# Forgetting attention and a GELU MLP on one core: four-head value products, weights loaded behind the first v, first scores by pairs of heads

## The chip, the cores and the metric

The kernel runs on one core of a Trainium2 chip. The metric is device time in microseconds (us). It is compared with the time of the kernel before the change on the same inputs. Engine names are those of the profile: PE is TensorE (PEld its weight loads), DVE is VectorE, ACT is ScalarE, POOL is GpSimd, SP is SyncE. SPq and POOLq are the sequencers of SP and POOL, which issue DMAs.

## The reference

Attention with a forget gate over 8 batches of 8 heads, 576 positions and 64 dims per head, followed by an MLP on the 4608 tokens, 512 wide, 2048 inside:

```python
scores = scale * np.matmul(q, k.transpose(0, 1, 3, 2))
log_f = np.log(np.clip(f, 0.0001, 1.0))
cum = np.cumsum(log_f, axis=-1)
decay = cum[:, :, :, None] - cum[:, :, None, :]
causal = np.triu(np.ones((S, S), dtype=bool), k=1)
scores = np.where(causal, -1000000000.0, scores + decay)
...
attn = attn / (np.sum(attn, axis=-1, keepdims=True) + 1e-09)
out = np.matmul(attn, v)
x = out.transpose(0, 2, 1, 3).reshape(B * S, H * D)
h = x @ w_in
g = 0.5 * h * (1.0 + np.tanh(c * (h + 0.044715 * h * h * h)))
return g @ w_out
```

The decay splits into a factor of the query, which cancels in the division, and a factor exp(-cum) of the key. The kernel multiplies v by that factor and sums it for the denominator.

## The kernel before

Four heads make a quad; there are 16 quads, two for each batch. For a quad, q and k arrive as bf16 through POOL's queue (`load_qk`) and DVE transposes them in 32 by 32 blocks of word pairs (`transpose_words`, L138), so that the 64 dims of a head lie as 32 partitions times two (the last index c of `qT` and `kT`). v arrives as f32 through SP's queue (`load_v`, L108), five DMAs for a batch; the first batch's v comes in two halves of four heads, ten DMAs.

`score_round` (L166) makes a third of a quad's causal scores: 512 columns for each of four heads, in two PSUM tiles of two heads each, and two exps on ACT (L186). A head's matmuls use 32 rows of PE, so four heads run side by side. `mask` (L188) zeroes the upper triangle on POOL. `make_vw` (L151) multiplies v by the key factor `wT` on POOL, and `copy_low` (L158) copies one 64-row block of it on DVE.

`denominators` (L223) multiplies the exps with the bf16 key factor in four column tiles of 32, one for each head. DVE transposes the result (L232), and for each of two head pairs x takes the reciprocal (L236), copies it to the other 32 partitions of each 64 (L239, two copies) and transposes it into `rb` (L241). `attn_out` (L245) makes the value product of the head pair x in two column tiles of 64, and DVE multiplies it by `rb` into `xT` (L249). All products share one PSUM buffer `po`; a product that is called `spare` takes one of the score buffers instead.

The MLP works in nine chunks of 512 tokens. `mlp_in` (L252) makes two blocks of 128 hidden units at a time from four row groups of w_in, with the gelu on ACT (L267). `mlp_out` (L269) is a generator: each step is one matmul of 128 by 512 (L274), 64 steps for a chunk, and each sixteenth is followed by a copy on DVE (L278) and a DMA to the output.

The order on every engine is written by hand. `setup` issues the first loads: f, k and q of quad 0, v of the first four heads, k and q of quad 1, v of the other four heads, and the four pieces of w_in on POOL's queue. `step(i, j, fill, fills)` goes through three rounds: the scores of quad i, then the denominators of quad j (round 0) or one of its two value products (rounds 1 and 2), then the vw and mask of quad i, then as many steps of `mlp_out` as `fills` says. Steps (0, None), (1, 0) and (None, 1) have no MLP work to fill with, since the first chunk needs the first batch's attention. w_out is issued after step 0, the second v after step 1 behind the last piece of w_in.

Of the kernel before, what the change touches and what calls it, by code (L numbers as in the profile page):

```python
# [16 lines left out]
def kernel(  # L17
# [93 lines left out]
            ))  # L111
        return ins

    w_in_hbm = moe_w_in.rearrange("(t p) n -> p t n", p=128)
    w_out_hbm = moe_w_out.rearrange("(t p) n -> p t n", p=128)

    def load_w_in(c):
        n = D_FF // 4
        return nc.gpsimd.dma_start(out=w_in_sb[:, :, n * c:n * (c + 1)],
                            in_=w_in_hbm[:, :, n * c:n * (c + 1)])  # L120

    def load_w_out(c):
        n = N_FT // 4
# [9 lines left out]
    def load_qk(i):  # L133
        return [load_one(k, k_c, i), load_one(q, q_c, i)]
# [10 lines left out]
    def transpose_k(i):  # L145
        transpose_words(k_c[i % 2], kT[i % 2][:, 64:64 + S])

    def transpose_q(i):
        transpose_words(q_c[i % 2], qT[i % 2])

    def make_vw(i):  # L151
        h0 = 4 * (i % QPB)
        vb = v_nat[(i // QPB) % 2]
        nc.gpsimd.tensor_mul(  # L154
            vw[i % 2][:, 0:NT], vb[:, :, h0:h0 + 4, :],
            wT[:, i, :, :].unsqueeze(3).to_broadcast([128, NT, 4, D]))
# [9 lines left out]
    def score_round(i, r):  # L166
        off, n = rounds[r]
        tiles = [psS.tile([128, 2, 512], FP32, name="ps_s", tag="s") for _ in range(2)]
        qq, p = qT[i % 2], pt[i % 2]
        parts = []  # L170
        for (key, col, q0, nq) in pieces:
            a, z = max(col, off), min(col + nq, off + n)
            if a < z:
                parts.append((key, a - off, q0 + a - col, z - a))
        for c in range(2):
            for j, (key, c0, q0, nq) in enumerate(parts):
                for h in range(4):
                    nc.tensor.matmul(  # L178
                        tiles[h // 2][:, h % 2, c0:c0 + nq],
                        key_columns(i, key, h, c),  # L180
                        qq[32 * h:32 * h + 32, q0:q0 + nq, c],
                        start=(c == 0 and j == 0), stop=(c == 1),
                        skip_group_check=True,
                    )
        for g in range(2):
            nc.scalar.activation(p[:, 2 * g:2 * g + 2, off:off + n], tiles[g], AF.Exp, scale=scale)  # L186

# [35 lines left out]
    def denominators(i):  # L223

        def column(h):

            return lambda t: (w_bf[:, i, t, h:h + 1] if t not in (0, LOW) else
                              w_bf[:, i, t, h:h + 1].to_broadcast([128, 32]))

        po = product(i, [(32 * g, column(h), h) for g, h in enumerate((0, 2, 1, 3))], False)  # L230
        den = den_pool.tile([128, S], FP32, name="den", tag="den")
        nc.vector.transpose(out=den, in_=po)  # L232

        for x in range(2):
            rec = den_pool.tile([128, S // 32], FP32, name=f"rec{x}", tag=f"rec{x}")
            nc.vector.reciprocal(rec, den[:, 0:S:32])  # L236
            for g in (0, 64):
                src, dst = g + 32 * x, g + 32 - 32 * x
                nc.vector.tensor_copy(rec[dst:dst + 32, :], rec[src:src + 32, :])  # L239
            rb = den_pool.tile([128, S], FP32, name=f"rb{x}", tag=f"rb{x}")  # L240
            nc.vector.transpose(out=rb.rearrange("p (c j) -> p c j", j=32),  # L241
                                in_=rec.unsqueeze(2).to_broadcast([128, S // 32, 32]))
            rbs[i, x] = rb

    def attn_out(i, x, spare=False):  # L245
        b, u = i // QPB, i % QPB
        po = product(i, [(64 * y, lambda t, h=2 * x + y: vw[i % 2][:, t, h, :], 2 * x + y)
                         for y in range(2)], spare)
        nc.vector.tensor_mul(xT[:, 2 * u + x, S * b:S * (b + 1)], po, rbs.pop((i, x)))  # L249


    def mlp_in(c, prs):  # L252
# [30 lines left out]

    def setup():
        nc.sync.dma_start(out=f_sb, in_=f.rearrange("b h s -> (b h) s"))
        load_qk(0)
        load_v(0, 0, 4)
        make_identity(nc, ident_f32)
        make_upper_triangular(nc, utri_f32, val=1.0, diag=True)
        load_qk(1)  # L290
        load_v(0, 4, 4)
        w_in_dmas.extend(load_w_in(c) for c in range(4))

        nc.vector.memset(ones_f32, 1.0)
        nc.vector.memset(logfT, 0.0)
# [45 lines left out]
    none = iter(())  # L341
    w_in_dmas = []

    def step(i, j, fill, fills):


        for r in range(3):
            if i is not None:
                score_round(i, r)
# [25 lines left out]

    with tc.manual_schedule():
        setup()
        step(0, None, none, (0, 0, 0))
        load_qk(2)
        w_out_dmas = [load_w_out(c) for c in range(4)]  # L380
        step(1, 0, none, (0, 0, 0))
        load_qk(3)
        v1 = load_v(1)
        after(v1[0], w_in_dmas[3])
        step(None, 1, none, (0, 0, 0))
        fill = none
        for c in range(NCH):

            mlp_in(c, (0, 1))
            for x in fill:  # L390
                pass
            if c == 0:
                prepare(2, 3)
                load_v(2)
            elif c + 1 < B:
                prepare(2 * c + 3, 2 * c + 4)
                if c + 2 < B:
                    load_v(c + 2)
# [46 lines left out]
```

## Time and profile before

| | us |
|---|---|
| median of 3 runs | 374.81 |
| lowest and highest | 371.65, 376.28 |
| the profiled execution | 373.05 |
| its span, first to last instruction | 371.3 |
| PE busy in the span | 335.7 (90%) |
| ACT busy | 188.9 (51%) |
| DVE busy | 152.4 (41%) |
| POOL busy | 108.3 (29%) |

The page cuts the span into 40 slices of 9.3 us and gives each engine's busy share in tenths; PEclk is the clock that PE was granted, in tenths of full speed. A row of a group of instructions reads: line, engine, operation, out<-in, shape, count | busy us, mean ns of one | idle time before them, with what ended it. In the timeline and the chain, a row begins with start and length in us. "x24" counts the instructions that were merged into the row.

### The profile page before, as it was taken

What the parts mean: (1) busy time and instruction counts of PE and PEld (TensorE: products, weight loads), DVE (VectorE), ACT (ScalarE), POOL (GpSimd) and SP (SyncE); (2) the same over time, 40 slices, a digit from 0 to 9 for tenths busy, and PEclk for the clock granted to TensorE, in tenths of its full rate; (3) what the DMA queues carried; (4) which work ended last, traced back from release to release, by engine and by line L of the source; (5) the groups of instructions that cost most, each with busy time, mean ns of one, the idle gap of its engine ahead of it and who ended that gap; (6) DMA issues with size and microseconds to landing.
All of it is one profiled execution on the core that took longest, in us unless ns stands there. A gap on an engine that the chain in (4) does not pass through costs nothing.

```text
span 371.3 us, 6656 instructions
## 1 busy us (share of the span) xinstructions
PE 335.7 (90%) x2825; PEld 153.8 (41%) x2825; DVE 152.4 (41%) x282; ACT 188.9 (51%) x188; POOL 108.3 (29%) x144
## 2 busy tenths in 40 slices
PE   0674898798999999999999999999999999999995
PEld 0322343344444444444444444444444444444442
DVE  5442802853455255525553545354533453001011
ACT  3661267736566556654755475547555642530510
POOL 6276122642415141524152415231540120000000
PEclk9855899989999999999999999999999999999999
DMA  8999992400940194018501860173010001002002
GB/s 157 197 206 197 218 215 73 65 30 31 194 90 30 56 189 95 30 58 179 106 31 58 163 122 31 57 157 63 30 58 28 2 30 57 28 2 85 28 33 82
DMA packets 51710, 33.09 MB, mean 89 GB/s; under 512 B 38816, under 2 KB 42912, under 8 KB 51680
## 3 DMA queue, kind: packets, MB, share of 16 engines
q0 software_dynamic: 8832, 13.63, 20.9%
q1 hardware_dynamic: 42848, 19.03, 20.1%
q8 instruction: 22, 0.36, 0.4%
q14 instruction: 8, 0.07, 0.1%
HBM read 36.85 MB, written 9.44 MB: 125 GB/s over the span
## 4 chain that ended last, share of the span: by engine, by line
PE 68%; DVE 12%; issue 7%; ACT 5%; SPq 4%; DMA 2%; POOL 2%; POOLq 0%; ACTq 0%
PE ps_h L260 33%; PE pso L274 23%; PE po L214 7%; PE ps_s L178 5%; ACT pt L186 5%; SPq L108 4%; DVE rec L239 3%; DVE rb L241 2%; DMA v_nat<-in_v_dram 2%; DVE xT L249 2%; DVE den L232 2%; DVE o_st L278 1%; DVE rec L236 1%; POOL vw L154 1%; POOL w_out_sb L124 1%
## 5 line engine op out<-in xcount | busy, mean ns | idle before, releaser
L274 PE MATMUL pso<-w_out_sb,gT 128*128 128x512 bf16 x576 | 135.3, 381 | 0.0
L260 PE MATMUL ps_h<-xT,w_in_sb 128*128 128x512 bf16 x576 | 127.7, 380 | 1.3 <-ACT gT L267 0.7
L267 ACT ACTIVATE gT<-ps_h 128x1024 bf16<-128x1024 f32 x72 | 72.8, 1023 | 104.2 <-PE ps_h L260 104.2
L186 ACT ACTIVATE pt<-ps_s 128x1024 bf16<-128x1024 f32 x96 | 93.0, 1021 | 51.6 <-PE ps_s L178 44.8
L260 PEld LDWEIGHTS <-w_in_sb 128*128 128x128 bf16 x576 | 56.4, 98 | 69.9 <-issue 2.3
L192 POOL TENSOR_SCALAR_AFFINE_SELECT pt<-pt 128x512 bf16<-128x512 bf16 (+2 forms) x80 | 46.8, 595 | 121.3 <-ACT pt L186 120.1
L274 PEld LDWEIGHTS <-gT 128*128 128x128 bf16 x576 | 52.8, 98 | 62.8 <-issue 1.7
L278 DVE COPY o_st<-pso 128x512 f32<-128x512 f32 x36 | 24.7, 687 | 91.8 <-PE pso L274 91.6
L178 PE MATMUL ps_s<-qT,kT 32*128 32x64 bf16 (+3 forms) x896 | 36.3, 271 | 12.3 <-ACT pt L186 8.3
L154 POOL TENSOR_TENSOR vw<-v_nat,wT 128x1280 bf16<-128x1280 f32 x16 | 37.3, 2334 | 19.3 <-DMA v_nat<-in_v_dram 14.7
L232 DVE STREAM_TRANSPOSE den<-po 128x576 f32<-128x576 f32 x16 | 12.5, 783 | 73.5 <-PE po L214 73.5
L214 PE MATMUL po<-pt,vw 128*64 128x512 bf16 (+1 forms) x360 | 28.9, 300 | 11.7 <-DVE xT L249 11.7
L178 PEld LDWEIGHTS <-kT 32*128 32x128 bf16 x896 | 16.4, 95 | 37.5 <-issue 30.8
L249 DVE TENSOR_TENSOR xT<-po,rb 128x576 bf16<-128x576 f32 x30 | 22.6, 755 | 20.3 <-PE po L214 20.1
L214 PEld LDWEIGHTS <-vw 128*64 128x64 bf16 x384 | 19.3, 118 | 26.3 <-issue 20.7
L241 DVE STREAM_TRANSPOSE rb<-rec 128x576 f32<-128x576 f32 x32 | 24.9, 778 | 1.1
L129 POOL DMA_DIRECT2D k_c<-in_k_dram x16 | 9.3, 582 | 46.9 <-DVE kT L138 46.1
L138 DVE STREAM_TRANSPOSE kT<-k_c 128x576 f32<-128x576 f32 x16 | 19.9, 1246 | 2.6 <-PE ps_s L178 1.5
L138 DVE STREAM_TRANSPOSE qT<-q_c 128x576 f32<-128x576 f32 x16 | 19.8, 1238 | 0.7 <-DMA q_c<-in_q_dram 0.7
L239 DVE COPY rec<-rec 32x18 f32<-32x18 f32 x64 | 17.0, 265 | 1.5
L214 PE MATMUL po<-pt,w_bf 128*32 128x64 bf16 (+5 forms) x384 | 15.9, 295 | 1.5 <-DVE xT L249 0.8
L186 ACT ACT_TABLE_LOAD x8 | 10.3, 1283 | 6.8 <-PE ps_s L178 6.8
(42 smaller groups left out, 61.6 us busy)
## 6 DMA issues: line engine op xcount, KB each, us to landing
out_dram<-o_st SPq DMA_DIRECT2D x36, 256.0 KB, 2.0
v_nat<-in_v_dram SPq DMA_DIRECT2D x28, 256.0 KB, 8.6
k_c<-in_k_dram POOLq DMA_DIRECT2D x16, 288.0 KB, 6.3
q_c<-in_q_dram POOLq DMA_DIRECT2D x16, 288.0 KB, 7.1
w_in_sb<-in_moe_w_in_dram POOLq DMA_DIRECT2D x4, 512.0 KB, 15.3
w_out_sb<-in_moe_w_out_dram POOLq DMA_DIRECT2D x4, 512.0 KB, 13.7
v_nat<-in_v_dram SPq DMA_DIRECT2D x15, 128.0 KB, 10.7
f_sb<-in_f_dram SPq DMA_DIRECT2D x1, 144.0 KB, 2.7
```

The costliest lines, as they stand in the source:

```text
L138: nc.vector.transpose(out=dst.rearrange("p s c -> p (s c)").bitcast(FP32) .rearrange("p (t a) -> p a t", a=S // 32), in_=src.rearrange("p ...
L154: nc.gpsimd.tensor_mul(vw[i % 2][:, 0:NT], vb[:, :, h0:h0 + 4, :], wT[:, i, :, :].unsqueeze(3).to_broadcast([128, NT, 4, D]))
L178: nc.tensor.matmul(tiles[h // 2][:, h % 2, c0:c0 + nq], key_columns(i, key, h, c), qq[32 * h:32 * h + 32, q0:q0 + nq, c], start=(c == 0 an ...
L186: nc.scalar.activation(p[:, 2 * g:2 * g + 2, off:off + n], tiles[g], AF.Exp, scale=scale)
L192: nc.gpsimd.affine_select(out=x, in_=x, compare_op=ALU.is_ge, fill=0.0, base=0, pattern=pattern, channel_multiplier=-1)
L214: nc.tensor.matmul(po[r0:r0 + w.shape[-1], 448 + q0:448 + q0 + nq], w, p[:, h, col:col + nq], start=(key in (0, "low")), stop=(key in ("lo ...
L241: nc.vector.transpose(out=rb.rearrange("p (c j) -> p c j", j=32), in_=rec.unsqueeze(2).to_broadcast([128, S // 32, 32]))
L249: nc.vector.tensor_mul(xT[:, 2 * u + x, S * b:S * (b + 1)], po, rbs.pop((i, x)))
L260: nc.tensor.matmul(ph[:, j, :], w_in_sb[:, dt, 128 * ft:128 * ft + 128], xT[:, dt, CH * c:CH * (c + 1)], start=(dt == 0), stop=(dt == N_DT ...
L267: nc.scalar.activation(gT[c % 2][:, 2 * pr:2 * pr + 2, :], ph, AF.Gelu_apprx_tanh)
L274: nc.tensor.matmul(pso, gT[c % 2][:, ft, 128 * n:128 * n + 128], w_out_sb[:, ft, :], start=(ft == 0), stop=(ft == N_FT - 1))
L278: nc.vector.tensor_copy(st, pso)
```

## The change

- `load_w_in` takes w_in in pieces of two row groups and half of the columns, where it took all four row groups and a quarter of the columns. Rows of w_in are read in pairs, so that row group 2u + x holds the rows of quad u whose dim has parity x, 32 rows for each of four heads.
- In `setup`, the first v waits for the first k. The first w_in piece waits for the eighth of the ten v DMAs (index 7). The other two w_in pieces are issued at the end of step 0, behind its last mask. k and q of quad 2 and the pieces of w_out go one after the other behind the three rounds of step 1. The second v waits for the third piece of w_out.
- `attn_out(i, x)` makes the product of all four heads with the dims of parity x, in four column tiles of 32. It uses 24 matmuls instead of 12. `denominators` makes one `rb` for the quad: the four copies, one reciprocal and one transpose go.
- `make_vw` of quads 0 and 1 runs on DVE. For later quads it stays on POOL, after the second mask instead of before the first, and `copy_low` follows in the third round.
- `score_round` of quads 0 and 1 makes its two PSUM tiles one after the other, two heads at a time.
- The counts of fills in the steps change.

```diff
-    w_in_hbm = moe_w_in.rearrange("(t p) n -> p t n", p=128)
+    w_in_hbm = moe_w_in.rearrange("(u p x) n -> p u x n", p=128, x=2)
...
-        n = D_FF // 4
-        return nc.gpsimd.dma_start(out=w_in_sb[:, :, n * c:n * (c + 1)],
-                            in_=w_in_hbm[:, :, n * c:n * (c + 1)])
+        n, u = D_FF // 2, c % 2
+        s = slice(n * (c // 2), n * (c // 2 + 1))
+        return nc.gpsimd.dma_start(out=w_in_sb[:, 2 * u:2 * u + 2, s], in_=w_in_hbm[:, u, :, s])
...
-    def make_vw(i):
+    def make_vw(i, eng):
...
-        nc.gpsimd.tensor_mul(
+        eng.tensor_mul(
...
-        for c in range(2):
-            for j, (key, c0, q0, nq) in enumerate(parts):
-                for h in range(4):
-                    nc.tensor.matmul(
...
+        for heads in ((0, 1), (2, 3)) if by_tile else (range(4),):
+            for c in range(2):
+                for j, (key, c0, q0, nq) in enumerate(parts):
+                    for h in heads:
+                        nc.tensor.matmul(
...
-        po = product(i, [(32 * g, column(h), h) for g, h in enumerate((0, 2, 1, 3))], False)
+        po = product(i, [(32 * h, column(h), h) for h in range(4)], False)
         den = den_pool.tile([128, S], FP32, name="den", tag="den")
         nc.vector.transpose(out=den, in_=po)
-        for x in range(2):
-            rec = den_pool.tile([128, S // 32], FP32, name=f"rec{x}", tag=f"rec{x}")
-            nc.vector.reciprocal(rec, den[:, 0:S:32])
-            for g in (0, 64):
-                src, dst = g + 32 * x, g + 32 - 32 * x
-                nc.vector.tensor_copy(rec[dst:dst + 32, :], rec[src:src + 32, :])
...
+        rec = den_pool.tile([128, S // 32], FP32, name="rec", tag="rec")
+        nc.vector.reciprocal(rec, den[:, 0:S:32])
+        rb = den_pool.tile([128, S], FP32, name="rb", tag="rb")
+        nc.vector.transpose(out=rb.rearrange("p (c j) -> p c j", j=32),
+                            in_=rec.unsqueeze(2).to_broadcast([128, S // 32, 32]))
+        rbs[i] = rb
...
-        po = product(i, [(64 * y, lambda t, h=2 * x + y: vw[i % 2][:, t, h, :], 2 * x + y)
-                         for y in range(2)], spare)
-        nc.vector.tensor_mul(xT[:, 2 * u + x, S * b:S * (b + 1)], po, rbs.pop((i, x)))
+        po = product(i, [(32 * h, lambda t, h=h: vw[i % 2][:, t, h, x:D:2], h) for h in range(4)], spare)
+        nc.vector.tensor_mul(xT[:, 2 * u + x, S * b:S * (b + 1)], po, rbs[i])
...
-        load_qk(0)
-        load_v(0, 0, 4)
+        k0 = load_qk(0)[0]
...
         load_qk(1)
-        load_v(0, 4, 4)
-        w_in_dmas.extend(load_w_in(c) for c in range(4))
+        v0 = load_v(0, 0, 4)
+        after(v0[0], k0)
+        v0 += load_v(0, 4, 4)
+        w_in_dmas.append(load_w_in(0))
+        after(w_in_dmas[0], v0[7])
+        w_in_dmas.append(load_w_in(1))
...
+        first = i is not None and i < 2
...
-                if r == 0:
-                    make_vw(i)
-                    if i == 0:
-                        transpose_k(1)
-                        transpose_q(1)
+                if i == 0 and r == 0:
+                    transpose_k(1)
+                    transpose_q(1)
+                if r == 0 and first:
+                    make_vw(i, nc.vector)
                     copy_low(i)
                 mask(i, r)
+                if r == 1 and not first:
+                    make_vw(i, nc.gpsimd)
+                if r == 2 and not first:
+                    copy_low(i)
+            if extra[r]:
+                extra[r]()
             pull(fill, fills[r])
...
-        step(0, None, none, (0, 0, 0))
-        load_qk(2)
-        w_out_dmas = [load_w_out(c) for c in range(4)]
-        step(1, 0, none, (0, 0, 0))
+        step(0, None, none, (0, 0, 0),
+             (None, None, lambda: w_in_dmas.extend(load_w_in(c) for c in (2, 3))))
+        w_out_dmas = []
+        step(1, 0, none, (0, 0, 0),
+             (lambda: load_qk(2),
+              lambda: w_out_dmas.extend(load_w_out(c) for c in (0, 1)),
+              lambda: w_out_dmas.extend(load_w_out(c) for c in (2, 3))))
         load_qk(3)
         v1 = load_v(1)
-        after(v1[0], w_in_dmas[3])
+        after(v1[0], w_out_dmas[2])
...
-                step(2, None, fill, (8, 6, 6))
+                step(2, None, fill, (9, 8, 7))
                 prepare(4)
-                step(3, 2, fill, (6, 6, 6))
+                step(3, 2, fill, (6, 6, 5))
...
-                step(i, i - 1, fill, (9, 8, 8))
-                step(i + 1 if i + 1 < NQ else None, i, fill, (8, 8, 8))
+                step(i, i - 1, fill, (12, 8, 8))
+                step(i + 1 if i + 1 < NQ else None, i, fill, (8, 7, 7))
```

More of the change, by code (lines that the diff above doesn't have):

```diff
@@ L164, in key_columns, with score_round @@
         return kT[i % 2][32 * h:32 * h + 32, 64 * b0:64 * b0 + 128, c]
-    def score_round(i, r):
+    def score_round(i, r, by_tile):
         off, n = rounds[r]
@@ L174, in score_round @@
                 parts.append((key, a - off, q0 + a - col, z - a))
-        for c in range(2):
-            for j, (key, c0, q0, nq) in enumerate(parts):
-                for h in range(4):
[L178 to L184, printed above, removed]
+        for heads in ((0, 1), (2, 3)) if by_tile else (range(4),):
[3 more added lines that the diff above has]
+                        nc.tensor.matmul(
+                            tiles[h // 2][:, h % 2, c0:c0 + nq],
+                            key_columns(i, key, h, c),
+                            qq[32 * h:32 * h + 32, q0:q0 + nq, c],
+                            start=(c == 0 and j == 0), stop=(c == 1),
+                            skip_group_check=True,
+                        )
         for g in range(2):
@@ L342, with step @@
     w_in_dmas = []
-    def step(i, j, fill, fills):
+    def step(i, j, fill, fills, extra=(None, None, None)):
+        first = i is not None and i < 2
         for r in range(3):
             if i is not None:
-                score_round(i, r)
+                score_round(i, r, first)
                 if i == 0 and r == 0:
```

4 lines of the change are left out of this document (removed).

## The prediction

> **What bounds the kernel now.** I read the page's slices first, then busy time by stage, then the chain of waits. The DMA engines' slices, each 9.3 us:
>
> ```profile
> DMA  8999992400940194018501860173010001002002
> ```
>
> They are full in the first six slices and never as long again. By stages (length; PE, weight loads, DVE, ACT, POOL busy; TensorE's granted clock; DMA share; GB/s):
>
> ```profile
> 0.00:40.83 40.83, 19.78 (x220) 9.60 (x220) 19.29 (x50) 16.75 (x18) 21.95 (x36) 0.71 1.11 190
> 55.20:92.30 37.10, 30.98 (x346) 14.08 (x344) 17.27 (x31) 22.77 (x23) 15.63 (x20) 0.95 0.23 53
> 74.40:77.80 3.40, 2.73 (x16) 1.34 (x16) 1.37 (x2) 0.00 (x0) 2.24 (x3) 0.50 0.22 82
> 92.30:129.80 37.50, 36.85 (x337) 16.94 (x336) 17.86 (x33) 22.48 (x23) 12.65 (x16) 1.00 0.41 92
> ```
>
> TensorE (PE) has three places to gain: the opening (40.83 us, PE half busy), chunk 0 (37.10 - 30.98 = 6.1 us idle, and 3.4 us at half clock), and 0.65 us in each later chunk. Everything else is PE work that the change doesn't lessen. The chain through the end of the opening (start, length, what):
>
> ```profile
> 28.92 2.34 POOL vw L154
> 31.72 0.77 DVE xT L249
> 32.53 1.56 PE po L214 x12
> ...
> 34.93 1.56 PE po L214 x13
> 36.51 0.79 DVE den L232
> ...
> 39.35 0.78 DVE rb L241
> ```
>
> It hangs on `make_vw(1)`, which starts only at 28.92. Why so late is told by the landing times (an issue, and the time from issue to landing, below it):
>
> ```profile
> L108 SPq DMA_DIRECT2D v_nat<-in_v_dram x1: 3210/3210/3210, 15.5 to 15.5; - x1
> ...
> DMA to landing us min/median/max: 13.2/13.2/13.2
> ```
> ```profile
> L119 POOL DMA_DIRECT2D w_in_sb<-in_moe_w_in_dram x4: 770/778/787, 4.6 to 6.8; - x4
> ...
> DMA to landing us min/median/max: 11.4/15.3/19.2
> ```
>
> The last piece of the first v lands at 15.5 + 13.2 = 28.7 us. The four w_in pieces, issued at 4.6 to 6.8, land from 16.0 to 26.0, in the same stretch: weights that nobody needs before 39 share the DMA engines with v.
>
> **The opening, rebuilt.** The other rows needed:
>
> ```profile
> 6.22 1.26 DVE L138 STREAM_TRANSPOSE kT<-k_c 128x576 f32<-128x576 f32 x1 [0.64 <-DMA k_c<-in_k_dram]
> ...
> 13.55 1.94 ACT L186 ACTIVATE pt<-ps_s 128x1024 bf16<-128x1024 f32 x2
> ...
> 15.32 1.24 DVE L138 STREAM_TRANSPOSE qT<-q_c 128x576 f32<-128x576 f32 x1
> ...
> 18.38 3.02 POOL L192 TENSOR_SCALAR_AFFINE_SELECT pt<-pt 64x256 bf16<-64x256 bf16 x5
> ...
> 21.76 1.04 PE L178 MATMUL ps_s<-qT,kT 32*128 32x64 bf16 x16
> ...
> 39.19 1.03 PE L260 MATMUL ps_h<-xT,w_in_sb 128*128 128x512 bf16 x2
> ```
>
> *Loads.* v now starts when the first k has landed (6.2 us: its transpose starts then). Ten v pieces follow with only q0, k1 and q1 beside them, then nothing. The nearest rows for the spacing of two pieces: the w_in pieces landed one every (19.2 - 11.4 + 2.2) / 3 = 3.3 us with v beside them, and the third v, almost alone, has pieces of twice the size issued and landed in 4 to 6 us, each issue taking 0.85 (its row stands with the rivals). I take 1.9 us for the first three pieces, between the two, and 0.9 after. The first half then lands near 13, piece 7 near 15.5 and the last near 17, against 28.7 now. Bounds for piece 7: 13 to 21.
>
> *POOL.* It waits in its own queue for piece 7 before the first w_in, and quad 0's masks stand behind that. Two issues (2 x 0.78) to 17.1, masks 3.02 to 20.1; now they end at 18.38 + 3.02 = 21.4, since `make_vw(0)` stands before them on POOL. So only 1.3 us is won here; what is late next is the masks, not v.
>
> *DVE.* It takes both `make_vw`. Its price isn't in the trace: 1.7 us scaled from xT's 0.77 in the chain (576 columns, here 1280), 2.34 at most, as on POOL, and 1.2 at least, the 1.24 of a transpose. The first stands behind quad 1's transposes, at 16.6 (15.32 + 1.24), its v landed; the second behind the reciprocal chain of quad 0, where only xT waits.
>
> *Scores by tile.* Two heads at a time stream as many columns as four side by side, so I charge each half of a round 0.95 us, near the whole round's 1.04. In return the first exp starts after half, and ACT's exps (1.94 a round) follow each other. In quad 0 the masks wait for POOL anyway, so I credit nothing; PE's extra time in quad 1 is in the walk.
>
> The walk: denominators(0) 20.1 to 21.7 on PE (1.56 by the chain, as for each product here); scores(1,1) to 23.5; value product (0,0) to 25.1; DVE meanwhile den, rec and rb to 23.5, vw(1) and copy_low to 25.6, xT to 26.4; scores(1,2) to 26.9; product (0,1) to 28.5 and xT to 29.25; mask(1,2) 29.2; denominators(1) to 30.8; products (1,0), (1,1) to 33.9; one rb instead of two has xT(1,0) done at 33.4, before the third w_in row group is wanted. The MLP starts at 33.9. Now it starts with two matmuls at 39.19 and then stands until 40.83, worth a start at 40.4 at full clock. I allow 0.7 us for half clock at the new start (0 to 1.7). **Opening: 40.4 - 34.6 = 5.8 us gained**, 2 to 8 with piece 7 at 21 or 13. The first two w_in land near 23, the next near 28, needed at 34 and 41. w_out, issued some 3 us later than now behind fewer bytes, lands near 43, needed at 49. Both cost nothing: the MLP's first 64 matmuls cover them.
>
> **Chunk 0.** Here DVE's chain stops PE. Rows, in order of time, then PE's waits from 55.2 to 92.3:
>
> ```profile
> 68.21 2.35 POOL L154 TENSOR_TENSOR vw<-v_nat,wT 128x1280 bf16<-128x1280 f32 x1
> ...
> 68.63 2.32 DVE L239 COPY rec<-rec 32x18 f32<-32x18 f32 x2
> ...
> 75.07 1.54 PE L214 MATMUL po<-pt,vw 128*64 128x512 bf16 x12 [2.87 <-DVE xT L249]
> ...
> 85.66 0.88 PE L214 MATMUL po<-pt,vw 128*64 128x512 bf16 x12 [0.99 <-DVE xT L249]
> ```
> ```profile
> PE po L214 <- DVE xT L249: 3.9, 2, 2.9
> PE ps_s L178 <- ACT pt L186: 2.3, 4, 0.7
> ```
>
> Two copies of 0.27 us took 2.32 us beside POOL's `make_vw`, and xT came late by 2.87. The change drops all four copies, one reciprocal and one rb transpose per quad, and moves `make_vw` behind mask 1. Both waits go: 3.9 us. The half clock in 74.40:77.80 follows the long one; 3.4 us at half is 1.7 us. Fills 9, 8, 7 for 8, 6, 6 put up to 0.2 + 0.4 + 0.2 us of PE work into waits for ACT; three fewer are left to cover the first gelu of the next chunk (0.1). **6.3 us**, 3 to 7.
>
> The Trainium skill, "SBUF — State Buffer", section "SBUF: two separate sides", says that VectorE and GpSimd share a port pair as an exclusive lock, also for a VectorE operation with both inputs in SBUF against a GpSimd read. The two copies above agree with the lock; `make_vw` on VectorE beside the masks isn't in this trace. By that rule the masks and it would hold each other up in the opening, by my estimate up to 1.7 us, and the sum would be that much less.
>
> **Later chunks.** PE's waits after 92.3, in six chunks:
>
> ```profile
> PE ps_s L178 <- ACT pt L186: 2.5, 6, 0.4
> PE po L214 <- DVE xT L249: 1.2, 5, 0.2
> ```
>
> 12 fills for 9 cover the 0.4 after ACT's table load (three matmuls of 1.83 / 8, below), and the shorter DVE chain most of the 0.2. POOL's `make_vw` (2.33) now lies between mask 1 and mask 2; a round is at least 0.6 + 0.8 + 1.8 = 3.2 us by the rows below and a mask about 0.6 (3.02 / 5), so 0.2 us is left: free, just. **3.0 us**, 0 to 3.7.
>
> **The value product.** Twice the matmuls, four heads in 32 columns each. The denominators already have that form, 24 in four column tiles. A round's scores, a product and eight fills of now, in the chain, and further on the denominators:
>
> ```profile
> 107.92 0.63 PE ps_s L178 x14
> 108.55 0.81 PE po L214 x12
> 109.36 1.83 PE pso L274 x8
> ...
> 152.52 0.83 PE po L214 x24
> ```
>
> 0.02 us more x 28 products at full clock: **0.6 us lost**. The bounds: nothing, and what the weight loads would cost unhidden. The row of the nearest ones:
>
> ```profile
> L214 PEld LDWEIGHTS <-w_bf 128*32 128x32 bf16 x128 | 2.1, 95 | 5.0 <-issue 4.0 <-DVE xT L249 1.1
> ```
>
> 24 x 95 ns would be 2.3 us; I take the denominators' row, as it is the same shape but for one-column weights in two thirds. Permuted w_in rows change no instruction of the MLP.
>
> **Sum:** 5.8 + 6.3 + 3.0 - 0.6 = 14.5 us, from the profiled execution's 373.05 (span 371.3) to 358.6. The median of the runs, 374.81, is 1.8 higher; 14.5 off that is 360.3. I put it between: **359.5 us**.
>
> **Rivals.**
> *The second v comes late.* It now waits for the third w_out, so it starts near 40.5 instead of 26, while PE wants it 6 us sooner. Its last piece, and the tail of the third v:
>
> ```profile
> L108 SPq DMA_DIRECT2D v_nat<-in_v_dram x1: 3617/3617/3617, 42.0 to 42.0; - x1
> ...
> DMA to landing us min/median/max: 11.8/11.8/11.8
> ```
> ```profile
> L108 SPq DMA_DIRECT2D v_nat<-in_v_dram x3: 835/852/3150, 50.5 to 54.6; - x3
> ...
> DMA to landing us min/median/max: 4.1/4.7/6.0
> ```
>
> It lands at 53.8 now. In the new order w_out is nearly done when it starts, k and q still run beside it; at 2.3 us a piece that is again near 54. `make_vw(2)` is due on POOL near 57, and mask(2,2) stands behind it. Past 57 each microsecond is one of PE; landing at 61 gives 363.5. Chance 0.13.
> *The opening doesn't shorten*, because v, delayed by k, reaches piece 7 only at 21 and POOL holds the masks: the change then doesn't do what it says there. 2 us or less are gained, 364. Against it: the weights are out of the way. Chance 0.12.
> *Issue of twice the matmuls.* The denominators' weight loads, as issued:
>
> ```profile
> 66.50 0.78 PEld L214 LDWEIGHTS <-w_bf 128*32 128x32 bf16 x24 [0.22 <-issue]
> ```
>
> If each of 12 more matmuls added its share of that, 33 ns, 0.39 x 28 = 11 us would go and 370 be left. The 0.83 row speaks against it. Chance 0.07.
> The Trainium skill, "TensorEngine Tiling (Array Packing)", section "Instruction Overhead", gives each matmul some 60 cycles; 12 more of them in 28 products would, as an estimate from that page, take about 8 us. The 0.83 us row doesn't show it.
> *Slower: strided 32-column loads that don't hide* under four short streams. The gain is gone at 0.5 us more per product (14.5 / 28), 2% slower from 0.8; at the bound of 2.3 us a product, 1.5 more, it would be 400. The scores' loads from kT already take every second element, and PE waits for none of them in the later chunks (the two waits there are quoted above). Chance 0.04.
>
> **Numbers.** Forecast 0.64 (354 to 363), the others as given. The range 354 to 366 takes in the first two rivals, 0.89 less the ends of each. A measurement of this kernel tells about 2% from no change, so faster means below 367.3: 0.64 + 0.13 + 0.10 = 0.87; within 2% 0.09; slower 0.04.
>
> **What would show it.** Right: the MLP's first matmul at 33 to 35; `make_vw(1)` on DVE below 26; no wait for xT over 0.3 us from 50 to 86 and no half clock there; products of 24 matmuls in 0.81 to 0.87. Wrong: POOL idle for the second v with PE waiting behind mask(2,2); masks of quad 0 ending after 22; products near 1.2.

## The result and the profile after

The changed kernel takes 356.57 us, the median of 4 runs (355.17 to 357.89), against 373.23 us (369.32 to 376.28). The ratio is 0.9587, with a 95% interval of 0.9487 to 0.9686: faster. Ratios here leave out executions that took over 1.5% more than the fastest of their kernel, so they are not quotients of the medians. Its profiled execution took 355.17 us with a span of 353.4.

The slices of PE and its granted clock before, then those of the changed kernel with the DMA engines below:

```profile
PE   0674898798999999999999999999999999999995
...
PEclk9855899989999999999999999999999999999999
```
```profile
PE   1778988999999999999999999999999999999995
...
PEclk9866999999999999999999999999999999999999
DMA  7799999507710671059113911280110011001011
```

The dip of the clock in the ninth slice (0.8, the 3.4 us at half clock in chunk 0) is gone, and PE is busy for eight tenths or more of every slice from the fourth on, but for the last. The stages are cut at the first matmul of the MLP, at the first of w_out, and at the first w_in matmuls of chunk 1; the last row is from chunk 2 to chunk 3. Before, then after (length; PE, weight loads, DVE, ACT, POOL busy; clock; DMA share; GB/s):

```profile
0.00:39.19 39.19, 18.75 (x217) 9.32 (x218) 17.68 (x47) 16.75 (x18) 21.95 (x36) 0.71 1.11 190
39.19:55.05 15.86, 14.57 (x69) 6.33 (x66) 6.97 (x8) 7.06 (x7) 3.19 (x5) 0.97 1.12 218
55.05:87.35 32.30, 26.18 (x324) 11.92 (x323) 17.27 (x30) 20.42 (x21) 15.17 (x20) 0.95 0.27 62
124.36:161.87 37.51, 36.86 (x337) 16.97 (x336) 17.87 (x32) 22.29 (x23) 12.66 (x17) 1.00 0.41 92
```
```profile
0.00:32.17 32.17, 19.08 (x265) 9.57 (x267) 18.85 (x40) 16.51 (x18) 17.67 (x34) 0.80 0.92 170
...
32.17:46.94 14.77, 14.04 (x63) 6.28 (x64) 4.72 (x5) 7.05 (x7) 1.58 (x3) 0.98 1.18 201
46.94:75.26 28.32, 25.30 (x370) 11.42 (x373) 11.97 (x18) 19.36 (x20) 15.38 (x19) 1.00 0.75 158
111.10:147.66 36.56, 35.87 (x378) 16.53 (x384) 14.76 (x21) 22.26 (x23) 12.62 (x17) 1.00 0.42 95
```

Up to the first matmul of w_out, 55.05 - 46.94 = 8.1 us are won; in chunk 0 32.30 - 28.32 = 4.0; in each of chunks 2 to 5 37.51 - 36.56 = 0.95, and 5.6 over chunks 1 to 6 together. The spans differ by 17.9; the 0.2 that is left lies in chunk 7. Some PE records are missing from the trace, so PE's busy times after are a little low; the stage lengths are not touched by that.

The opening of the changed kernel in the timeline:

```profile
15.55 1.41 POOL L120 DMA_DIRECT2D w_in_sb<-in_moe_w_in_dram  x2 [10.74 <-DMA v_nat<-in_v_dram]
15.94 1.48 DVE L154 TENSOR_TENSOR vw<-v_nat,wT 128x1280 bf16<-128x1280 f32 x1
...
16.97 3.33 POOL L193 TENSOR_SCALAR_AFFINE_SELECT pt<-pt 64x256 bf16<-64x256 bf16 x5
...
22.61 1.58 DVE L154 TENSOR_TENSOR vw<-v_nat,wT 128x1280 bf16<-128x1280 f32 x1
...
24.79 0.76 DVE L244 TENSOR_TENSOR xT<-po,rb 128x576 bf16<-128x576 f32 x1
```

POOL waits 10.7 us for piece 7 of v and goes on at 15.55; the masks follow at once and end at 20.3. vw(1) starts at 22.6, where it started at 28.9. What ended PE's idle time in chunk 0 now:

```profile
56.59 2.33 POOL L154 TENSOR_TENSOR vw<-v_nat,wT 128x1280 bf16<-128x1280 f32 x1 [0.76 <-DMA v_nat<-in_v_dram]
...
58.41 0.62 PE L215 MATMUL po<-pt,w_bf 128*32 128x512 bf16 x12
...
59.56 0.31 PE L215 MATMUL po<-pt,w_bf 128*1 128x320 bf16 x4 [0.53 <-POOL pt L193]
60.15 0.28 PE L215 MATMUL po<-pt,w_bf 128*1 128x192 bf16 x8 [0.28 <-POOL pt L193]
```

The 2.87 us wait for xT is gone. In its place the denominators of quad 2 come in three parts, because POOL waited for the second v before vw(2), and the last masks stand behind that.

### The profile page after: what moved, and what is told of

Same layout as the page of the kernel before. It is cut to its first block, busy times and chain, and to the rows that moved or that the text cites. A ratio compares the mean times of both kernels' runs of the same rounds, so it can differ in the third digit from the quotient of the medians.

```text
span 353.4 us, 7265 instructions
## 1 busy us (share of the span) xinstructions
PE 327.9 (93%) x3156; PEld 150.8 (43%) x3209; DVE 128.1 (36%) x188; ACT 188.6 (53%) x188; POOL 103.9 (29%) x142
## 3 DMA queue, kind: packets, MB, share of 16 engines
q0 software_dynamic: 7808, 13.63, 22.2%
## 4 chain that ended last, share of the span: by engine, by line
PE 77%; DMA 8%; POOL 5%; SPq 4%; issue 2%; DVE 1%; another core or an unknown queue 1%; ACT 0%; POOLq 0%
PE ps_h L255 31%; PE pso L269 31%; PE po L215 8%; PE ps_s L179 6%; SPq L108 4%; DMA w_out_sb<-in_moe_w_out_dram 4%; DMA v_nat<-in_v_dram 3%; POOL pt L193 2%; POOL vw L154 1%; DMA k_c<-in_k_dram 1%; POOL w_in_sb L120 1%; POOL w_out_sb L124 0%; DVE kT L138 0%; DVE qT L138 0%
## 5 line engine op out<-in xcount | busy, mean ns | idle before, releaser
L269 PE MATMUL pso<-w_out_sb,gT 128*128 128x512 bf16 x534 | 128.7, 379 | 4.4 <-issue 3.3
L255 PEld LDWEIGHTS <-w_in_sb 128*128 128x128 bf16 x576 | 56.4, 98 | 69.3 <-issue 2.2
L244 DVE TENSOR_TENSOR xT<-po,rb 128x576 bf16<-128x576 f32 x30 | 22.7, 757 | 37.5 <-PE po L215 37.3
L154 POOL TENSOR_TENSOR vw<-v_nat,wT 128x1280 bf16<-128x1280 f32 x14 | 32.6, 2327 | 0.8 <-DMA v_nat<-in_v_dram 0.8
L179 PEld LDWEIGHTS <-kT 32*128 32x128 bf16 x896 | 16.5, 94 | 31.5 <-issue 25.4
L215 PE MATMUL po<-pt,vw 128*32 128x512 bf16 (+1 forms) x720 | 27.4, 289 | 1.4 <-DVE xT L244 1.2
L215 PEld LDWEIGHTS <-vw 128*32 128x32 bf16 x768 | 16.3, 101 | 16.6 <-issue 9.6
L237 DVE STREAM_TRANSPOSE rb<-rec 128x576 f32<-128x576 f32 x16 | 12.5, 778 | 0.5
L215 PEld LDWEIGHTS <-w_bf 128*1 128x1 bf16 (+1 forms) x384 | 7.3, 89 | 12.3 <-issue 6.3
```

What stands on the lines that cost most here:

```text
L154: eng.tensor_mul(vw[i % 2][:, 0:NT], vb[:, :, h0:h0 + 4, :], wT[:, i, :, :].unsqueeze(3).to_broadcast([128, NT, 4, D]))
L179: nc.tensor.matmul(tiles[h // 2][:, h % 2, c0:c0 + nq], key_columns(i, key, h, c), qq[32 * h:32 * h + 32, q0:q0 + nq, c], start=(c == 0 an ...
L215: nc.tensor.matmul(po[r0:r0 + w.shape[-1], 448 + q0:448 + q0 + nq], w, p[:, h, col:col + nq], start=(key in (0, "low")), stop=(key in ("lo ...
L255: nc.tensor.matmul(ph[:, j, :], w_in_sb[:, dt, 128 * ft:128 * ft + 128], xT[:, dt, CH * c:CH * (c + 1)], start=(dt == 0), stop=(dt == N_DT ...
L269: nc.tensor.matmul(pso, gT[c % 2][:, ft, 128 * n:128 * n + 128], w_out_sb[:, ft, :], start=(ft == 0), stop=(ft == N_FT - 1))
```

## The experiments

All are edits of the changed kernel. Each was timed against the kernel before on the same chip; ratios are to that kernel. Stages are cut as above, from the profiled execution of each.

**The order of loads (two runs).** First all four w_in pieces in the setup, nothing else:

```diff
-        after(w_in_dmas[0], v0[7])
-        w_in_dmas.append(load_w_in(1))
+        w_in_dmas.extend(load_w_in(c) for c in (1, 2, 3))
...
-             (None, None, lambda: w_in_dmas.extend(load_w_in(c) for c in (2, 3))))
+             (None, None, None))
```

> The changed kernel with all four w_in pieces issued in the setup, waiting for nothing; the rest (v behind the first k, w_out and quad 2 between the rounds of step 1, the second v behind the third w_out) stays. With the whole old order the first v landed at 38.7, which w_in, k, q and w_out did together. Theory (any weights queued beside v hold it up, packet by packet): the w_in pieces land at 14 to 25, the first v's last piece at 22 to 28 instead of 16, vw(1) on DVE and the first xT follow it, MLP start at 33.5 to 38, total 358 to 363. Rival (only the early w_out hurt; v has landed before anything needs it): MLP start at 30.5 to 32.5 as in the changed kernel, total within 1.5 us of 356.6.

363.10 us, ratio 0.9759 (0.9678 to 0.984). The profiled execution took 365.90, the longest of the four (the shortest took 361.14); in it the MLP starts at 43.88, later than in the kernel before. From its timeline:

```profile
24.39 1.49 DVE L154 TENSOR_TENSOR vw<-v_nat,wT 128x1280 bf16<-128x1280 f32 x1 [8.30 <-DMA v_nat<-in_v_dram]
...
34.91 1.49 DVE L154 TENSOR_TENSOR vw<-v_nat,wT 128x1280 bf16<-128x1280 f32 x1 [6.84 <-DMA v_nat<-in_v_dram]
...
37.50 1.53 PE L215 MATMUL po<-pt,vw 128*32 128x512 bf16 x24 [7.97 <-DVE xT L244]
```

Both vw wait for v, the second until 34.9. The theory holds: weights beside v hold it up. In this execution its size was set too low: v landed at 34.7, not by 28.

Then the whole old order: the first v waits for no k, and w_out and the second v are issued as before too:

```diff
-        after(v0[0], k0)
...
-        after(w_in_dmas[0], v0[7])
-        w_in_dmas.append(load_w_in(1))
+        w_in_dmas.extend(load_w_in(c) for c in (1, 2, 3))
...
-             (None, None, lambda: w_in_dmas.extend(load_w_in(c) for c in (2, 3))))
-        w_out_dmas = []
-        step(1, 0, none, (0, 0, 0),
...
+        load_qk(2)
+        w_out_dmas = [load_w_out(c) for c in range(4)]
+        step(1, 0, none, (0, 0, 0))
...
-        after(v1[0], w_out_dmas[2])
+        after(v1[0], w_in_dmas[3])
```

> The changed kernel with its loads in the old order: v of the first batch from the start, all four w_in pieces (in the new shape) issued in the setup, k, q and w_out issued between step 0 and step 1, the second v behind the last w_in. Theory (weights on the same DMA engines hold up v): the last piece of the first v lands at 23 to 28 us instead of 16.5, vw(1) follows it, the first xT comes 2 to 5 us later than 24.8, and the MLP starts at 34.5 to 37.5 instead of 32.2; total 358 to 361. Rival (vw on DVE and the scores by tile won the opening, the order of loads nothing): MLP start at or below 32.7, total 355 to 357.5. For the second v: it lands well before vw(2) is due, so the denominators of quad 2 take 1.0 us at most and chunk 0 after the first gelu is 1 to 1.5 us shorter than in the changed kernel.

367.30 us, ratio 0.9813 (0.9709 to 0.9916); the profiled execution, with 369.90 the longest of its four, starts the MLP at 47.78. The first v's last piece, from issue to landing:

```profile
L108 SPq DMA_DIRECT2D v_nat<-in_v_dram x1: 2922/2922/2922, 23.4 to 23.4; - x1
...
DMA to landing us min/median/max: 15.3/15.3/15.3
```

It lands at 38.7. Chunk 0 took 27.5 us in both runs, 0.8 less than in the changed kernel: the MLP starts so late that the second v has landed by the time it is wanted. The two profiles are long ones, so the size is better taken from the ratios: 0.9759 and 0.9813 against 0.9587 are some 6.4 and 8.4 us of the 373, and with the 0.8 us won back in chunk 0 the openings are some 7 and 9 us longer. So with vw on DVE and everything else new, little or nothing of the opening's 8.1 us is left without the new order of loads.

**vw of quads 0 and 1 back on POOL.**

```diff
-                    make_vw(i, nc.vector)
+                    make_vw(i, nc.gpsimd)
```

> The changed kernel with vw of quads 0 and 1 on POOL (2.33 us each) instead of DVE (1.5 us). Theory (POOL's masks are what the denominators wait for): the masks of quad 0 end 2 to 2.5 us later than 20.3, those of quad 1 2.5 to 4.5 us later than 27.4, and the MLP starts 2 to 4 us later than 32.2; total 358.5 to 361. Rival (DVE or the loads set the end of the opening): MLP start within 0.7 us of 32.2, total within 1 us.

357.75 us, ratio 0.9588 (0.952 to 0.9656). The masks of quad 0 end at 21.7 instead of 20.3, those of quad 1 at 31.1 instead of 27.4, and the MLP starts at 34.09 instead of 32.17: the direction of the theory, but two of the three sizes lie just below its ranges. Up to w_out this execution takes 2.7 us more and in chunk 0 0.6 less (27.72), 2.1 in all (357.27 against 355.17). The medians differ by 1.2 us and the ratios not at all, so a cost in the total, forecast at 358.5 to 361, is not shown.

**Scores of quads 0 and 1 of all four heads at once.**

```diff
-                score_round(i, r, first)
+                score_round(i, r, False)
```

> The changed kernel with the scores of quads 0 and 1 of all four heads together, as before. The prediction's theory (in quad 0 the masks wait for POOL anyway, in quad 1 PE's doubled time and ACT's earlier start cancel): MLP start within 0.5 us of 32.2, total within 1 us. Rival (ACT's exps are the opening's bound): the exps of quads 0 and 1 stand 0.7 us apart again, the last one ends 1.5 to 2.5 us later than 25.5, and the MLP starts as much later; total 358 to 359.

356.36 us, ratio 0.9536 (0.945 to 0.9622): no difference in time. The MLP started at 29.64 in this profile, but at 31.59 and 31.80 in two further kernels with the same edit (below), and between 30.77 and 32.17 in the five with the scores by tile and the same opening. PE's granted clock from 12 to 29 us was 1.00 in this profile and 0.71 to 0.76 in the five, but 1.00 and 0.65 in the two further ones, so the clock alone doesn't sort them either. The two ways can't be told apart, and so the scores by pairs of heads are not shown to win anything. What the run did show is chunk 0:

```profile
56.63 2.33 POOL L154 TENSOR_TENSOR vw<-v_nat,wT 128x1280 bf16<-128x1280 f32 x1 [2.70 <-DMA v_nat<-in_v_dram]
...
59.61 0.43 PE L215 MATMUL po<-pt,w_bf 128*1 128x320 bf16 x4 [2.48 <-POOL pt L193]
```

The MLP started 2.5 us sooner, yet vw(2) starts at 56.6 as before, PE stands 2.5 us behind its masks, and the clock is near half (0.57) for 6.8 us after that. Chunk 0 took 32.6 us: the sooner start is lost there.

**The value product as before**, with the denominators' tail and the row order of w_in:

```diff
...
-        po = product(i, [(32 * h, lambda t, h=h: vw[i % 2][:, t, h, x:D:2], h) for h in range(4)], spare)
-        nc.vector.tensor_mul(xT[:, 2 * u + x, S * b:S * (b + 1)], po, rbs[i])
+        po = product(i, [(64 * y, lambda t, h=2 * x + y: vw[i % 2][:, t, h, :], 2 * x + y)
+                         for y in range(2)], spare)
+        nc.vector.tensor_mul(xT[:, 2 * u + x, S * b:S * (b + 1)], po, rbs.pop((i, x)))
```

> The changed kernel with the value product, the denominators' tail on DVE and the row order of w_in as before; loads, scores, vw and fills stay changed. Theory (DVE's chain behind the denominators is what PE waits for): four copies, a reciprocal and a transpose come back, 1.6 to 2.1 us a quad. The MLP of chunk 0 starts 1.5 to 3 us later than 32.2; chunk 0 gets 1 to 4 us longer; PE again waits for xT in the later chunks, 0.2 to 0.3 us each. Total 360 to 364. Rival (DVE is busy for a third of the span and hides this; the loads made all the gain): all stages within 0.5 us of the changed kernel, total 356 to 358. Second rival (24 matmuls in 32 columns cost more than 12 in 64): the products get shorter by more than 0.05 us each, and the later chunks with them.

361.05 us, ratio 0.9674 (0.9603 to 0.9744). Up to w_out it takes 49.98 instead of 46.94 (3.0), chunk 0 31.49 instead of 28.32 (3.2). PE's waits in these two stages, before the end of chunk 0:

```profile
PE po L215 <- DVE xT L250: 2.5, 2, 1.9
PE ps_h L261 <- DVE xT L250: 1.6, 1, 1.6
```

They are waits for xT again. But the later chunks take 36.59 us, 0.03 more than with the new product: there DVE's chain costs next to nothing. The first theory holds for the first two stages only. The second rival falls, since twice the matmuls cost no more: 0.80 us for the 24 of a product in the changed kernel's chain, 0.81 for the 12 of this one.

**Where the later chunks' 0.95 us come from (three runs).** The fills as before; vw and copy_low of later quads in round 0 as before; that together with the old product:

```diff
-                step(i, i - 1, fill, (12, 8, 8))
-                step(i + 1 if i + 1 < NQ else None, i, fill, (8, 7, 7))
+                step(i, i - 1, fill, (9, 8, 8))
+                step(i + 1 if i + 1 < NQ else None, i, fill, (8, 8, 8))
```
```diff
-                if r == 0 and first:
-                    make_vw(i, nc.vector)
+                if r == 0:
+                    make_vw(i, nc.vector if first else nc.gpsimd)
                     copy_low(i)
                 mask(i, r)
-                if r == 1 and not first:
-                    make_vw(i, nc.gpsimd)
-                if r == 2 and not first:
-                    copy_low(i)
```

(In the first of the three, chunk 0 had its old fills too.)

> The changed kernel with the counts of fills as before. The value product undone left the later chunks at 36.59 us against 36.57, so the 0.94 us won in each is not DVE's. Theory (the three more fills cover the first exp): the wait of 0.6 us after the first round comes back, each later chunk takes 37.1 to 37.3 us; chunk 0 0.3 to 0.9 us longer; total 4 to 5 us more. Rival (vw behind the second mask, and copy_low out of the way of xT, made most of it): later chunks at 36.6 to 36.9.

> The changed kernel with vw and copy_low of quads 2 and later in round 0 ahead of the first mask, as before. Theory: in chunk 0 all masks of quad 2 then stand behind the second v, the masks are 3 us late, and PE stands 3 to 5 us for them: total 3 to 6 us more. In the later chunks copy_low stands ahead of xT again: 0 to 0.3 us a chunk. Rival (the place of vw makes no difference, PE has fills enough): total within 1 us, all chunks within 0.1 us.

> The changed kernel with the value product and DVE's chain as before, and also vw and copy_low of later quads in round 0 as before. In the later chunks the old fills give back 0.61 of the 0.94 us, the old product alone 0.02, the old place of vw alone 0. Theory (either of the two is enough to have xT in time, only both late make PE wait): later chunks at 36.8 to 36.95 us. Rival (the rest belongs to the fills too, or to nothing of these): 36.6. Chunk 0 has the waits of both: 33 us or more; total 364 to 368.

Totals 359.84 (0.9649, 0.9587 to 0.9711), 358.67 (0.9627, 0.9576 to 0.9677) and 362.14 us (0.9753, 0.9695 to 0.981), all three below what was expected. The same later chunk in each, in this order:

```profile
113.18:150.35 37.17, 36.18 (x379) 16.66 (x385) 14.09 (x21) 22.28 (x23) 12.63 (x17) 1.00 0.41 93
```
```profile
114.36:150.92 36.56, 35.87 (x378) 16.51 (x384) 14.30 (x20) 22.27 (x23) 12.68 (x17) 1.00 0.42 95
```
```profile
118.40:154.99 36.59, 35.90 (x332) 16.68 (x336) 17.96 (x32) 22.27 (x23) 12.66 (x17) 1.00 0.42 95
```

With the new fills a later chunk takes 36.6 us whatever product, DVE chain or place of vw it has; with the old fills 37.2 beside the new ones and 37.5 beside the old ones. So once the new fills are there, the rest wins 0.03 at most, and the third run's theory falls. How the fills can end a wait for xT too is in DVE's order: each sixteenth fill is followed by a copy on DVE. Before, that copy stood ahead of the xT that PE waited for; in the third run, with the same product and place of vw, it comes behind it:

```profile
195.27 0.69 DVE L278 COPY o_st<-pso 128x512 f32<-128x512 f32 x1
...
195.88 0.75 DVE L249 TENSOR_TENSOR xT<-po,rb 128x576 bf16<-128x576 f32 x1
...
196.68 0.88 PE L214 MATMUL po<-pt,vw 128*64 128x512 bf16 x12 [0.24 <-DVE xT L249]
```
```profile
188.37 0.76 DVE L250 TENSOR_TENSOR xT<-po,rb 128x576 bf16<-128x576 f32 x1
...
189.04 0.68 DVE L279 COPY o_st<-pso 128x512 f32<-128x512 f32 x1
```

In chunk 0 the old ways cost more. With the old fills it took 30.0 us, 1.7 more than in the changed kernel, where 0.3 to 0.9 was expected: PE waited 2.5 us for exps instead of 1.4 and 1.2 for masks instead of 0.8. With the old place of vw it took 32.7 us: vw(2) waited 9.0 us for the second v with every mask of quad 2 behind it, and PE stood 3.3 us for those.

**The second v (three runs).** It waits for the first w_out instead of the third; the same with whole score rounds; and k and q of quad 5 loaded after the third mask of quad 2:

```diff
-        after(v1[0], w_out_dmas[2])
+        after(v1[0], w_out_dmas[0])
```
```diff
-                prepare(2, 3)
+                prepare(2, 3, late=(5,))
...
-                step(2, None, fill, (9, 8, 7))
+                step(2, None, fill, (9, 8, 7), (None, None, lambda: load_qk(5)))
```

> The changed kernel with the second v waiting for the first w_out piece instead of the third. Theory (the second v's landing is what chunk 0 waits for: in the changed kernel it lands at 56.4, vw(2) stands on POOL for it and mask(2,2) behind that): v starts about 5 us sooner and lands at 52 to 54.5; the two halves of the denominators of quad 2 are no longer apart by 0.8 us, chunk 0 from the first second-layer matmul to the first matmul of chunk 1 takes 27.0 to 27.7 us instead of 28.3. The last w_out lands up to 3 us later than 43, before 49, and costs nothing. Total 0.6 to 1.3 us less. Rival (chunk 0 is bound by ACT's exps and the order on DVE, v comes in time): chunk 0 within 0.3 us of 28.3.

> The scores of quads 0 and 1 of all four heads together, and the second v behind the first w_out piece. With the first alone the MLP started 2.5 us sooner, at 29.6, but PE then stood 2.5 us behind mask(2,2) and ran 6.8 us at half clock, since the second v landed at 56.5 whatever came before. Theory (the second v is what ends chunk 0): with both, MLP start at 29.2 to 30.2, the second v at 52 to 54.5, chunk 0 28.5 us or less, total 2.5 to 4 us below the changed kernel. Rival (the sooner start is lost to something else, such as the third k or w_out): total within 1 us of the changed kernel.

> The changed kernel with k and q of quad 5 loaded after the third mask of quad 2 instead of ahead of quad 2's masks. Starting the second v 5 us sooner didn't make it land sooner (57.0 against 56.4), so the queue as a whole is what it waits for: until about 55 k and q of quads 3 to 5 go through the same DMA engines. Theory (bytes ahead of the second v's end): 0.59 MB less ahead of it, at some 195 GB/s 3 us; v lands at 53 to 54.5, POOL doesn't wait for it, the wait of PE behind mask(2,2) goes (0.8 us in the changed kernel, up to 2.7 in the runs where the MLP started sooner), chunk 0 27.0 to 27.8 us; total 0.5 to 2 us less. Rival (something else than bytes holds the second v, such as its own small packets): it lands within 0.7 us of 56.4, total the same.

The first gave 356.98 us (0.9573, 0.9522 to 0.9625), the second 356.88 (0.9583, 0.9528 to 0.9637). In the first, v was issued 6 us sooner (34.4 instead of 40.7) and landed no sooner: vw(2) starts at 57.17,

```profile
57.17 2.33 POOL L154 TENSOR_TENSOR vw<-v_nat,wT 128x1280 bf16<-128x1280 f32 x1 [2.67 <-DMA v_nat<-in_v_dram]
...
60.14 0.31 PE L215 MATMUL po<-pt,w_bf 128*1 128x320 bf16 x4 [2.45 <-POOL pt L193]
```

and chunk 0 took 31.5 us. In the second v landed at 56.9 and chunk 0 took 30.9. Here the theory that the landing is the bound holds, and the means to shift it did not work. Quad 5's k and q out of the way did. That kernel took 353.08 us (352.99 to 353.43), ratio 0.9509 (0.9461 to 0.9557). In its timeline:

```profile
54.53 2.33 POOL L154 TENSOR_TENSOR vw<-v_nat,wT 128x1280 bf16<-128x1280 f32 x1
...
57.08 0.75 PE L215 MATMUL po<-pt,w_bf 128*32 128x512 bf16 x16
...
58.10 0.28 PE L215 MATMUL po<-pt,w_bf 128*1 128x192 bf16 x8 [0.26 <-POOL pt L193]
```

v landed at 54.4 (48.9 + 5.4 in its landing row), before POOL wanted it, and chunk 0 took 27.58 us. The first of the three reached w_out at the same time (45.6 in both) and had v only at 57.0, so a shorter opening doesn't explain the 2.6 us. This kernel is the fastest of all: no run of it overlaps with one of the changed kernel. The two intervals of the ratio do overlap, and 1.3 us of its lead are a shorter opening, which the edit doesn't touch. What is shown is the landing and the 0.7 us in chunk 0.

**Both k and q of quads 4 and 5 late**, with whole score rounds, and quad 4's transposes in step 3:

```diff
-                step(2, None, fill, (9, 8, 7))
-                prepare(4)
-                step(3, 2, fill, (6, 6, 5))
+                step(2, None, fill, (9, 8, 7), (None, lambda: load_qk(4), lambda: load_qk(5)))
+                step(3, 2, fill, (6, 6, 5), (None, lambda: prepare(4), None))
```

> Scores of quads 0 and 1 of all four heads together; k and q of quad 4 loaded behind vw(2) on POOL, those of quad 5 after quad 2's third mask, and quad 4's transposes moved from after step 2 into step 3. Theory: with neither of the two loads ahead of it the second v lands at 50 to 52.5, so the MLP's sooner start (29.6 to 30.5) is kept: no wait over 0.5 us and no half clock in chunk 0, 27 to 28 us for it; total 2.5 to 4.5 us below the changed kernel. Rival (the sooner start is lost to something else, such as the late k of quad 4 before step 4): PE stands over 1 us before the scores of quad 4, total within 1 us of the changed kernel.

356.28 us, ratio 0.9597 (0.9537 to 0.9658). v landed at 53.3, but the two DMA issues of quad 4's k and q, 0.6 us each on POOL, stood ahead of mask(2,2): PE waited 2.2 us for masks and 0.9 for xT, and chunk 0 took 29.65 us. Neither theory nor rival named this; the v was freed and the order on POOL gave it back.

## Why the prediction was right

The range held, the sign was right, and the opening and chunk 0 won by the mechanisms that were named. The sum was 14.5 us on the profiled execution; that execution gave 17.9. That it came so near is in part luck: two terms were too small by 2.3 and 2.6 us and a third too large by 2.3. One of the named signs of being wrong did show, in small: POOL idle for the second v with PE behind mask(2,2). The terms, one by one:

*Opening, 5.8 forecast, 8.1 measured.* The mechanism is shown by the two runs on the loads, the masks as what is late next by the run with vw on POOL. The landings were close: piece 7 near 15.5 in the forecast, POOL released at 15.55; the last piece near 17, landed at 16.5. The size was off in the walk behind it. The denominators of quad 0 were to start when the masks end; they started at 18.47, beside the masks, and ended at 20.7, forecast 21.7. The next round of scores took 1.0 us, not 1.8, and the first product 1.29, not 1.56. So the walk was 2.2 us ahead at 22.9, and 1.7 of that was left when the MLP started at 32.17, forecast 33.9. The MLP then ran at half clock only until 32.8, which cost 0.3 us where 0.7 had been allowed.

*Chunk 0, 6.3 forecast, 4.0 measured.* The waits for xT and the half clock went, as forecast. The term failed in "again near 54" for the second v: it landed at 56.4, while POOL was ready for it at 55.8, sooner than the 57 of the forecast since the opening had become shorter. The denominators of quad 2 then took 60.43 - 58.41 = 2.0 us instead of 0.8. This is the first rival, in small: 1.2 us. Another 0.65 us is work that moved in: chunk 0 now holds 61 fills instead of 58, chunk 1 two fewer and chunk 7 one fewer. The remaining 0.4 us is not accounted for.

*Later chunks, 3.0 forecast, 5.6 measured,* of which 0.4 are the two fills that chunk 1 no longer holds. The step "12 fills for 9 cover the 0.4 ... and the shorter DVE chain most of the 0.2" named one right cause and one wrong. The new fills give 0.61 a chunk with the new DVE chain and 0.92 with the old one; the DVE chain gives 0.03 once the fills are there. The waits that the profile listed, 0.4 and 0.2, were also two thirds of what they cost: from the start of the second round's scores to that of its product it was 1.17 us before (107.31 to 108.48) and is 0.57 after (168.54 to 169.11); in the last round it was 0.87 and is 0.56.

*The value product, 0.6 lost forecast, nothing measured.* In the chain of the changed kernel:

```profile
165.12 0.80 PE po L215 x24
165.91 0.16 issue
166.07 2.54 PE pso L269 x11
168.61 0.57 PE ps_s L179 x16
169.18 0.80 PE po L215 x24
```

The first is a set of denominators, the second a value product, both of 24. The 0.83 row of the forecast included a gap: in the timelines 24 matmuls take 0.87 us, both the denominators before and the new value products, and the 12 of a value product before took 0.88. The overhead per matmul that the prediction cited from the Trainium skill ("TensorEngine Tiling (Array Packing)", "Instruction Overhead") doesn't show: no run here has a product that grew with its count. The rival of unhidden weight loads falls by the same rows.

*The port lock* of the cited section was priced at up to 1.7 us and took 0.3 at the first vw, because little lay side by side: it ran beside masks from 16.97 to 17.42 only, and the first mask took 0.72 us instead of 0.41. In the run whose second v waits for the first w_out, the same mask lies beside vw for 0.84 us and takes 1.12:

```profile
15.71 1.48 DVE L154 TENSOR_TENSOR vw<-v_nat,wT 128x1280 bf16<-128x1280 f32 x1
```
```profile
16.35 1.12 POOL L193 TENSOR_SCALAR_AFFINE_SELECT pt<-pt 64x256 bf16<-64x256 bf16 x1
```

With the whole old order of loads a mask that takes 0.66 us elsewhere starts just behind a vw of 1.49 us and takes 1.98. The first vw takes 1.48 or 1.49 us in all three, so the mask pays for nearly all of the overlap, as the section's exclusive lock has it. So the price holds where vw lies beside masks for its whole length, and this order of work hardly puts it there.

## What to carry to other kernels

Read from landing times which loads share the engines with the one that is waited for, and count the bytes ahead of its last piece: here, starting a load sooner helped nothing as long as the same bytes went beside it, and moving 0.59 MB behind it did. A stage that becomes shorter moves the need for its successors' loads forward, so the landing of each next load belongs into the forecast. An issue on POOL stands in the order of POOL's work: two of them ahead of a mask gave back what a sooner landing had won. When a wait is short and has several causes in one queue, undo them singly and together before one of them gets the credit.

## What the runs showed of the hardware

*Two queues share the DMA engines by packets, not bytes.* The changed w_in pieces have half as many packets: the software queue counts 7808 packets for the same 13.63 MB, 8832 before. Beside the old pieces a 128 KB piece of v landed about every 3.3 us (19.3 and 22.6). Beside the new ones, with the w_in pieces at the old place:

```profile
L108 SPq DMA_DIRECT2D v_nat<-in_v_dram x1: 417/417/417, 5.8 to 5.8; - x1
...
DMA to landing us min/median/max: 11.5/11.5/11.5
```
```profile
L108 SPq DMA_DIRECT2D v_nat<-in_v_dram x1: 1373/1373/1373, 6.3 to 6.3; - x1
...
DMA to landing us min/median/max: 17.0/17.0/17.0
```
```profile
L120 POOL DMA_DIRECT2D w_in_sb<-in_moe_w_in_dram x4: 698/708/717, 4.6 to 6.7; - x4
...
DMA to landing us min/median/max: 9.6/12.8/16.4
```

v pieces land at 17.3 and 23.3, 6.0 us apart, while w_in pieces land every (16.4 - 9.6 + 2.1) / 3 = 3.0. At 256 bytes a packet of v, 512 packets of v went in the time of two w_in pieces of 256 each: one for one. The packet records of the traces say the same: from 12 to 20 us v's queue started 751 packets beside 752 of the weights' queue with the new pieces, and 1255 beside 1256 in the kernel before. The Trainium skill, "DMA: Bandwidth & Descriptors", section "Queues, rings and completion order", says that each engine goes round its queues at packet granularity, where a packet is a bundle of descriptors. The equal counts agree with turns of equal length; how much one turn takes, no run here shows. Larger weight packets beside small ones make the small ones slower here, which is a reason why the old order cost the new kernel more than the kernel before; no run has the old pieces in the changed kernel, so that it is the only one is not shown.

*The same opening varies.* In the five kernels with identical instructions up to the MLP, it starts between 30.77 and 32.17 us. A single profile can't tell 1 us there.
